# Second SBUF tensors of a router search turned into per-partition scalars, and two of its small results kept in PSUM

## The chip, the cores and the metric

The kernel runs on one core of a Trainium2 chip. The metric is the device time of one execution in microseconds (us), as the median of several runs. The engines are TensorE (PE; its weight loads are PEld), VectorE (DVE), ScalarE (ACT), GpSimd (POOL) and SyncE (SP, which issues DMAs).

## The reference

Three layers run one after the other over 8 x 576 = 4608 tokens of 512 numbers. The first is banded attention with 8 heads. The second is a mixture of 8 experts, in which each token goes to the expert with its largest logit. The third, with which the change has to do, is a balanced mixture: no expert takes more than 4608 / 8 = 576 tokens, and the (token, expert) pairs are taken in falling order of their logits:

```
logits = x @ w_gate
order = np.argsort(-logits.flatten())
for idx in order:
    tok, e = int(idx) // E, int(idx) % E
    if assigned[tok] >= 0 or counts[e] >= cap:
        continue
    assigned[tok] = e
    counts[e] += 1
for e in range(E):
    mask = assigned == e
    h = np.maximum(x[mask] @ w1[e], 0.0)
    out[mask] = h @ w2[e]
```

## The kernel before

The tokens' logits for the third layer lie in SBUF as `lg`, 128 partitions x 40 columns x 8 experts. The greedy order is not walked pair by pair. Instead the kernel searches, eight times, for the logit at which the next expert becomes full, and fixes that expert's tokens. One such round is a `Phase`, numbered k from 0 to 7, and has these parts:

- `head`: the largest logit of each token, `m`, over the experts still open (line 1253); where it stands, `eq` (line 1256); `m` is then pushed below everything for tokens already assigned by adding `pen` (line 1257); `eq` times `rvc` (line 1259) and a maximum give the chosen expert `rm`, and `oh` (line 1269) its one-hot form. `wt` (line 1265) holds the step widths.
- `search`, six steps: `edges` (line 1278) writes 32 thresholds `ed` into a PSUM tile "pg"; `cm` (line 1297) compares `m` with them in two pieces; TensorE counts with `cm` and `oh` (line 1308), adds over column groups (line 1317) and over experts (line 1323). VectorE turns the counts into the number `nb` of thresholds passed (line 1327) and the new lower end `lo` (line 1333). The upper end is `tighten`: lines 1283, 1284 and 1286 compute `q`, and line 1288 takes the minimum into `hi`. These last four are handed out one by one in the next step.
- `route` fixes the expert `code` and its mark `cl` (line 1381), and finds each token's place with two products on TensorE.
- `settle` takes the expert out: `remb` (lines 1417 and 1419) counts the room left. `slots` turns the places into the list `idx` of the expert's tokens (lines 1425 to 1459), with `rr` (lines 1436, 1442), `bl` (line 1440), a product into "pt" (line 1448), its copy `sv` (line 1451), and a second product (line 1454).

Phase 0 runs while the second layer ends. Phases 1 to 7 run inside the third layer's matrix products: expert j is computed by `job2(j)` while the search for a later expert goes on between its matmuls. The order is fixed when the program is built: a clock that counts matmul time (`CLK`) and the costs that each part yields decide after which matmul the next small instruction is placed, and each engine executes its own sequence in order. The weights of the third layer are split into two parts, `wh` on ScalarE (line 202) and `wl` on GpSimd (line 203, a subtraction of two SBUF tensors of 128 x 512). GpSimd also issues the gathers of token rows (line 275) and the scatters of results (line 1548). VectorE makes the low part of the hidden layer, `ht` (line 880), and of the gathered rows, `xtl` (line 844), between the pieces of the search.

Of the kernel before, what the change touches and what calls it, by code (L numbers as in the profile page):

```python
# [10 lines left out]
F32 = mybir.dt.float32  # L11
# [5 lines left out]
OP = mybir.AluOpType  # L17
AX = mybir.AxisListType
# [139 lines left out]
def kernel(  # L158
# [1033 lines left out]
    def route_tables():  # L1192
# [13 lines left out]
        G.tensor_scalar(KC[3], cs[:, None, C_IOTA:C_IOTA + 32].to_broadcast([128, C, 32]), -1.0, 1.0, op0=OP.mult, op1=OP.mult)  # L1206
        G.tensor_copy(KC[4], cs[:, C_ROW:C_ROW + C])

    class Phase:
        def __init__(self, k):  # L1210
            self.k, self.tiles, self.lo, self.late = k, {}, lo0[:, 1:2], iter(())
# [8 lines left out]
    def head(T, c0=0):  # L1220
        V, k = nc.vector, T.k
        T.lo, T.late = lo0[:, 1:2], iter(())
        wt = T([128, NSTEP], "wt")
        df = T([128, 1], "df")
        if k == 0:
            m, rm, oh = top, TOP["rm"], TOP["oh"]
            V.memset(hi, BIG)
            s2 = T([128, 2], "s2")
            V.tensor_reduce(s2[:, 0:1], lmax, axis=AX.X, op=OP.max)
            V.tensor_reduce(s2[:, 1:2], lmin, axis=AX.X, op=OP.min, negate=True)  # L1230
            yield VP, 150
            p = pm2.tile([128, 128], F32, name="pr")
            nc.tensor.transpose(p[0:2, :], s2, ident)
            yield PE, 100
            fs = list(best(c0, C))
            for f in fs[:2]:
                f()
            v2 = T([2, 1], "v2")
            V.tensor_reduce(v2, p[0:2, :], axis=AX.X, op=OP.max)
            dg = T([2, 2], "dg")  # L1240
            V.tensor_scalar(dg, ident[0:2, 0:2], v2, None, op0=OP.mult)
            yield VP, 500
            p = pm2.tile([128, 128], F32, name="pr")
            nc.tensor.matmul(p[:, 0:2], onef[0:2, :], dg, start=True, stop=True)
            yield PE, 20
            for f in fs[2:]:
                f()
            V.tensor_scalar(lo0, p[:, 0:2], -1.0, None, op0=OP.mult)
            V.tensor_scalar(df, p[:, 0:1], lo0[:, 1:2], NWAY / (NWAY - 1.0), op0=OP.subtract, op1=OP.mult)
        else:  # L1250
            rvc, rve = KC[0], KC[1]
            m = T([128, C], "m")
            V.tensor_reduce(m, lg, axis=AX.X, op=OP.max)
            yield V, 400
            eq = T([128, 8 * C], "eq", F16).rearrange("p (c e) -> p c e", e=8)
            V.tensor_tensor(eq, lg, bC8(m), op=OP.is_equal)
            V.tensor_tensor(m, m, pen, op=OP.add)  # L1257
            yield V, 470
            V.tensor_tensor(eq, eq, rvc[:, None, :].to_broadcast([128, C, 8]), op=OP.mult)
            V.tensor_scalar(df, hi, lo0[:, 1:2], None, op0=OP.subtract)  # L1260
            yield V, 340
            rm = T([128, C], "rm", F16)
            with nc.allow_low_precision(reason="small whole numbers"):
                V.tensor_reduce(rm, eq, axis=AX.X, op=OP.max)
        V.tensor_scalar(wt, cs[:, C_PW:C_PW + NSTEP], df, None, op0=OP.mult)
        yield V, 500
        if k:
            oh = T([128, 8, C], "oh2", F16)
            V.tensor_tensor(oh, rve, rm[:, None, :].to_broadcast([128, 8, C]), op=OP.is_equal)
            yield V, 240  # L1270
        T.m, T.rm, T.oh, T.wt = m, rm, oh, wt
        if k < 7:
            edges(T, 0)
            yield V, 110

    def edges(T, s):
        T.ed = pm2.tile([128, NWAY], F32, name="pg")
        nc.vector.tensor_scalar(T.ed, cs[:, C_IOTA:C_IOTA + NWAY], T.wt[:, s:s + 1], T.lo, op0=OP.mult, op1=OP.add)

    def tighten(T, nb, w, lo):  # L1280
        V = nc.vector
        q = T([128, 2], "q")
        V.tensor_scalar(q[:, 0:1], nb, 1.0, w, op0=OP.add, op1=OP.mult)
        V.tensor_scalar(q[:, 1:2], nb, NWAY - 1.5, BIG, op0=OP.is_ge, op1=OP.mult)
        yield V, 200
        V.scalar_tensor_tensor(q[:, 0:1], q[:, 0:1], lo, q[:, 1:2], op0=OP.add, op1=OP.add)
        yield V, 130
        V.tensor_tensor(hi, hi, q[:, 0:1], op=OP.min)

    def search(T, s):  # L1290
        V, k, lo, ed, m, oh, late = nc.vector, T.k, T.lo, T.ed, T.m, T.oh, T.late
# [38 lines left out]
            V.scalar_tensor_tensor(T.sat, p[:, 0:8], nb, rev8, op0=OP.is_equal, op1=OP.mult)  # L1330
        yield V, YN[0]
        lo2 = T([128, 1], f"lo{s % 2}")
        V.scalar_tensor_tensor(lo2, nb, w, lo, op0=OP.mult, op1=OP.add)  # L1333
        T.late, T.lo = tighten(T, nb, w, lo), lo2
        yield V, YN[1]
        if s < NSTEP - 1:
# [3 lines left out]
    def route(T):  # L1340
# [36 lines left out]
        tot = T([2 * C, 128], "tot", F16)  # L1377
        nc.scalar.copy(tot, p[0:2 * C, :])
        if k < 7:
            cl = T([128, 8], "cl")  # L1380
            V.tensor_scalar(cl, rev8, code, None, op0=OP.is_equal)
            yield V, 80
            ck = T([128, 8], "ck")
            V.tensor_scalar(ck, cl, -2.0 * BIG, BIG, op0=OP.mult, op1=OP.add)
            yield V, 250
        else:
            yield PE, 300
# [138 lines left out]
    def split2(k, half):  # L1526
        j, q = pieces[k]
        loads2(k)
        w2nd.split(j, q, half)
        if half:  # L1530
            nsp[0] += 1
            loads2()
# [267 lines left out]
    for q in range(QFIRST, 4):  # L1800
        for h in range(2):
            split2(q, h)
    t0 = CLK[0]
    while CLK[0] < t0 + AHEAD:
        advance(0)
# [26 lines left out]
```

## Time and profile before

| What | Value |
|---|---|
| Median of 3 runs | 1314.62 us (1313.16 to 1315.28) |
| The profiled execution, its own time | 1317.96 us |
| Its span, first to last instruction | 1316.2 us |
| PE busy | 1225.6 us (93%) |
| DVE busy | 910.1 us (69%) |
| POOL busy | 546.5 us (42%) |
| ACT busy | 502.8 us (38%) |
| Mean granted TensorE clock | 0.975 |

A share of busy time is a mean over three layers with different limits. To see what the search costs one has to look at the stretch in which it runs, at what TensorE waits for there, and at the instructions in front of those waits.

### The profile page before, as it was taken

How to read it: one execution, taken by the hardware profiler on the slowest of the kernel's cores; microseconds unless marked ns; L12 is line 12 of the kernel's file. 1: busy time of each engine (PE TensorE's matmuls, PEld its weight loads, DVE VectorE, ACT ScalarE, POOL GpSimd, SP SyncE). 2: the span in 40 equal slices, each digit the busy share in tenths (PEclk: the TensorE clock that was granted, in tenths of full speed). 3: DMA queues.
4: the chain of work that ended last, by engine and by line, in shares of the span. 5: the costliest groups of instructions: out<-in, count | busy, mean ns of one | idle time of the engine just before them, and what ended most of it. 6: DMA issues, size and time to landing. Idle time of an engine off the chain costs nothing. (4 is left out here: it accounts for less than half of the span.)

```text
span 1316.2 us, 25338 instructions
## 1 busy us (share of the span) xinstructions
PE 1225.6 (93%) x9286; PEld 1045.1 (79%) x9286; DVE 910.1 (69%) x2702; ACT 502.8 (38%) x1388; POOL 546.5 (42%) x682
## 2 busy tenths in 40 slices
PE   7999999898899999999999969999989999999996
PEld 6887888687798978888888748687878788788894
DVE  5777778757999999977966547677677776752120
ACT  4666666433233342334333123232323332333330
POOL 4232222236435362543634024454555454446431
PEclk9999999888999999999999989899999999999998
DMA  9977676255424352433520050505050515054101
GB/s 204 218 186 176 154 176 147 78 185 195 147 84 140 105 156 87 149 105 106 164 87 1 21 175 17 182 19 174 28 180 21 160 42 180 22 180 149 68 5 36
DMA packets 157746, 155.07 MB, mean 118 GB/s; under 512 B 74296, under 2 KB 123320, under 8 KB 157488
## 3 DMA queue, kind: packets, MB, share of 16 engines
q1 hardware_dynamic: 148656, 124.50, 33.0%
q0 software_dynamic: 8960, 28.89, 7.2%
q8 instruction: 76, 1.25, 0.4%
q14 instruction: 54, 0.44, 0.1%
HBM read 124.46 MB, written 28.90 MB: 117 GB/s over the span
## 5 line engine op out<-in xcount | busy, mean ns | idle before, releaser
L203 POOL TENSOR_TENSOR wl<-wst,wh 128x512 fp32r<-128x512 f32 x250 | 323.9, 1318 | 276.2 <-ACT wh L202 268.6
L874 PE MATMUL ph<-xth,wh 128*128 128x256 f32 (+5 forms) x1024 | 314.2, 307 | 21.1 <-DVE ht L880 20.2
L874 PE MATMUL ph<-xtl,wh 128*128 128x256 f32 (+5 forms) x1024 | 309.9, 303 | 0.3 <-DVE xtl L844 0.3
L874 PE MATMUL ph<-xth,wl 128*128 128x256 f32 (+5 forms) x1024 | 309.2, 302 | 0.0
L900 PE MATMUL py<-wh,ht 128*128 128x512 f32 (+2 forms) x848 | 282.0, 409 | 1.3 <-DVE jk L942 1.3
L878 ACT ACTIVATE ht<-ph 128x256 fp32r<-128x256 f32 (+5 forms) x256 | 106.7, 417 | 297.7 <-PE ph L874 297.5
L874 PEld LDWEIGHTS ph<-xth,wh 128*128 128x128 f32 x1024 | 194.9, 190 | 29.7 <-DVE ht L880 24.1
L880 DVE SCALAR_TENSOR_TENSOR ht<-ph,ht 128x256 fp32r<-128x256 f32 (+4 forms) x344 | 124.1, 382 | 107.8 <-ACT ht L878 103.5
L874 PEld LDWEIGHTS ph<-xtl,wh 128*128 128x128 f32 x1024 | 195.0, 190 | 2.4 <-DVE xtl L844 0.5
L874 PEld LDWEIGHTS ph<-xth,wl 128*128 128x128 f32 x1024 | 194.8, 190 | 1.5
L900 PEld LDWEIGHTS py<-wh,ht 128*128 128x128 f32 (+2 forms) x848 | 157.2, 190 | 39.4 <-issue 4.1
L900 PE MATMUL py<-wl,ht 128*128 128x512 f32 (+2 forms) x424 | 172.4, 407 | 0.0
L202 ACT CAST wh<-wst 128x512 fp32r<-128x512 f32 x256 | 148.1, 618 | 9.6 <-SPq L1638 5.9
L436 POOL TENSOR_TENSOR pr<-pr,st 128x384 f32<-128x384 f32 x68 | 56.2, 826 | 145.6 <-DVE st L434 82.4
L426 ACT ACTIVATE pr<-pS,st 128x96 f32<-128x96 f32 x288 | 94.2, 341 | 55.3 <-DVE st L430 26.7
L1548 POOL DMA_INDIRECT out_dram<-xo,tki x40 | 41.2, 1029 | 158.1 <-ACT xo L910 39.8
L844 DVE TENSOR_TENSOR xtl<-pt,xth 128x512 fp32r<-128x512 f32 (+1 forms) x78 | 50.0, 646 | 82.1 <-ACT xth L843 78.1
L900 PEld LDWEIGHTS py<-wl,ht 128*128 128x128 f32 (+2 forms) x424 | 80.7, 190 | 21.3 <-issue 3.2
L942 DVE SCALAR_TENSOR_TENSOR jk<-py,aux,wgb 128x512 f32<-128x512 f32 (+2 forms) x128 | 95.6, 747 | 2.8
L415 PEld LDWEIGHTS pS<-kt,qb 128*128 128x128 f32 x576 | 75.1, 195 | 8.3 <-POOL qb L629 2.9
L910 ACT COPY xo<-py 128x512 f32<-128x512 f32 (+1 forms) x40 | 23.4, 585 | 149.8 <-issue 73.4
L415 PE MATMUL pS<-kt,qb 128*128 128x96 f32 x576 | 75.6, 275 | 3.9 <-DVE qb L389 2.8
(310 smaller groups left out, 2006.8 us busy)
## 6 DMA issues: line engine op xcount, KB each, us to landing
wst<-in_moe_w_dram SPq DMA_DIRECT2D x132, 512.0 KB
x_d<-xo SPq DMA_DIRECT2D x34, 257.0 KB
x_d<-xr SPq DMA_DIRECT2D x8, 1028.0 KB
knp<-in_k_dram SPq DMA_DIRECT2D x32, 128.0 KB
qnp<-in_q_dram SPq DMA_DIRECT2D x32, 128.0 KB
vd<-in_v_dram SPq DMA_DIRECT2D x8, 384.0 KB
wgb<-wg_d SPq DMA_DIRECT2D x1, 2048.0 KB
vp<-in_v_dram SPq DMA_DIRECT2D x12, 168.0 KB
```

What stands on the lines that cost most here:

```text
L202: nc.scalar.copy(h[:, s], t[:, s])
L203: (self.eng0 if (j, q) in self.early else self.eng).tensor_tensor(l[:, s], t[:, s], h[:, s].bitcast(F32), op=OP.subtract)
L415: nc.tensor.matmul(p[:, u, :], QB[a][hp][:, 4 * g + u].rearrange("p h c -> p (h c)"), win, start=False, stop=True, skip_group_check=True)
L426: nc.scalar.activation(pr[:, u], sm[:, u], AF.Exp, bias=st[:, 1, u:u + 1], accum_out=st[:, 2, u:u + 1])
L436: eng.tensor_tensor(pr, pr, st[:, 3, :, None].to_broadcast([128, 4, 96]), op=OP.mult)
L844: nc.vector.tensor_sub(l[:, :, o], p[:, :, :m], h[:, :, o].bitcast(F32))
L874: nc.tensor.matmul(p[:, :n], a, b[:, c, o:o + n], start=(k == 0), stop=(k == 11))
L878: nc.scalar.activation(h.hi[:, o:o + n], p[:, :n], AF.Relu)
L880: nc.vector.scalar_tensor_tensor(lo, p[:, a - o:b - o], 0.0, h.hi[:, a:b].bitcast(F32), op0=OP.max, op1=OP.subtract)
L900: nc.tensor.matmul(p[:m], h.part[a][:, 128 * t:128 * t + m], w_, start=(f == 0 and w_ is wh and a == 0), stop=(f == 7 and w_ is wl))
L942: nc.vector.scalar_tensor_tensor(JK[e % 2][:m], a, s, WG["b"][:m, e], op0=OP.mult, op1=OP.mult, accum_out=lt[:m, e:e + 1])
L1548: st = nc.gpsimd.indirect_dma_start(out=out, out_offset=bass.IndirectOffsetOnAxis(ap=ti[:m], axis=0), in_=xo[:m, 0:DM], in_offset=None)
```

## The change

Three things are done, all of them on VectorE:

- `lo`, `q` and `hi` (lines 1333, 1286 and 1288) had one-element tensors as their second tensor. They become `tensor_scalar` instructions, in which the second operand is a scalar read per partition. This holds for all phases.
- One PSUM tile, `RS[0]`, takes the buffer "pg" when the third layer begins and keeps it to the end. For phases 1 to 7 the thresholds lie in it, in two halves that the steps use in turn, the maxima `m0` in columns 64 to 103, and the mark `cl` in columns 104 to 111. `m`, the sum with `pen`, stays in SBUF.
- So `eq` and `m` read `m0`, and `remb` reads `cl`, from PSUM.

```diff
@@ -1206,6 +1206,8 @@
         G.tensor_scalar(KC[3], cs[:, None, C_IOTA:C_IOTA + 32].to_broadcast([128, C, 32]), -1.0, 1.0, op0=OP.mult, op1=OP.mult)
         G.tensor_copy(KC[4], cs[:, C_ROW:C_ROW + C])
 
+    RS = []
+
     class Phase:
         def __init__(self, k):
             self.k, self.tiles, self.lo, self.late = k, {}, lo0[:, 1:2], iter(())
@@ -1249,12 +1251,12 @@
             V.tensor_scalar(df, p[:, 0:1], lo0[:, 1:2], NWAY / (NWAY - 1.0), op0=OP.subtract, op1=OP.mult)
         else:
             rvc, rve = KC[0], KC[1]
-            m = T([128, C], "m")
-            V.tensor_reduce(m, lg, axis=AX.X, op=OP.max)
+            m, m0 = T([128, C], "m"), RS[0][:, 64:64 + C]
+            V.tensor_reduce(m0, lg, axis=AX.X, op=OP.max)
             yield V, 400
             eq = T([128, 8 * C], "eq", F16).rearrange("p (c e) -> p c e", e=8)
-            V.tensor_tensor(eq, lg, bC8(m), op=OP.is_equal)
-            V.tensor_tensor(m, m, pen, op=OP.add)
+            V.tensor_tensor(eq, lg, bC8(m0), op=OP.is_equal)
+            V.tensor_tensor(m, m0, pen, op=OP.add)
             yield V, 470
             V.tensor_tensor(eq, eq, rvc[:, None, :].to_broadcast([128, C, 8]), op=OP.mult)
             V.tensor_scalar(df, hi, lo0[:, 1:2], None, op0=OP.subtract)
@@ -1274,7 +1276,8 @@
             yield V, 110
 
     def edges(T, s):
-        T.ed = pm2.tile([128, NWAY], F32, name="pg")
+        o = NWAY * (s % 2)
+        T.ed = RS[0][:, o:o + NWAY] if T.k else pm2.tile([128, NWAY], F32, name="pg")
         nc.vector.tensor_scalar(T.ed, cs[:, C_IOTA:C_IOTA + NWAY], T.wt[:, s:s + 1], T.lo, op0=OP.mult, op1=OP.add)
 
     def tighten(T, nb, w, lo):
@@ -1283,9 +1286,9 @@
         V.tensor_scalar(q[:, 0:1], nb, 1.0, w, op0=OP.add, op1=OP.mult)
         V.tensor_scalar(q[:, 1:2], nb, NWAY - 1.5, BIG, op0=OP.is_ge, op1=OP.mult)
         yield V, 200
-        V.scalar_tensor_tensor(q[:, 0:1], q[:, 0:1], lo, q[:, 1:2], op0=OP.add, op1=OP.add)
+        V.tensor_scalar(q[:, 0:1], q[:, 0:1], lo, q[:, 1:2], op0=OP.add, op1=OP.add)
         yield V, 130
-        V.tensor_tensor(hi, hi, q[:, 0:1], op=OP.min)
+        V.tensor_scalar(hi, hi, q[:, 0:1], None, op0=OP.min)
 
     def search(T, s):
         V, k, lo, ed, m, oh, late = nc.vector, T.k, T.lo, T.ed, T.m, T.oh, T.late
@@ -1330,7 +1333,7 @@
             V.scalar_tensor_tensor(T.sat, p[:, 0:8], nb, rev8, op0=OP.is_equal, op1=OP.mult)
         yield V, YN[0]
         lo2 = T([128, 1], f"lo{s % 2}")
-        V.scalar_tensor_tensor(lo2, nb, w, lo, op0=OP.mult, op1=OP.add)
+        V.tensor_scalar(lo2, nb, w, lo, op0=OP.mult, op1=OP.add)
         T.late, T.lo = tighten(T, nb, w, lo), lo2
         yield V, YN[1]
         if s < NSTEP - 1:
@@ -1377,7 +1380,7 @@
         tot = T([2 * C, 128], "tot", F16)
         nc.scalar.copy(tot, p[0:2 * C, :])
         if k < 7:
-            cl = T([128, 8], "cl")
+            cl = RS[0][:, 64 + C:72 + C] if k else T([128, 8], "cl")
             V.tensor_scalar(cl, rev8, code, None, op0=OP.is_equal)
             yield V, 80
             ck = T([128, 8], "ck")
@@ -1800,6 +1803,7 @@
     for q in range(QFIRST, 4):
         for h in range(2):
             split2(q, h)
+    RS.append(pm2.tile([128, 512], F32, name="pg"))
     t0 = CLK[0]
     while CLK[0] < t0 + AHEAD:
         advance(0)
```

The change moves no instruction: each engine's sequence is the one of before, with other operands on VectorE. Two places show it. The first is VectorE in the head of phase 2, behind the product "pt" that `sv` copies; the names are those of the list above, and `po`, `df` and `kpad` are small helpers. Before:

```order
L1419 SCALAR_TENSOR_TENSOR remb<-cl,remb 128x8
L1253 TENSOR_REDUCE m<-lg 128x40
L1256 TENSOR_TENSOR eq<-lg,m 128x320
L1257 TENSOR_TENSOR m<-m,pen 128x40
L1451 CAST sv<-pt 128x36
L1259 TENSOR_TENSOR eq<-eq,rvc 128x320
L1260 TENSOR_SCALAR df<-hi,lo_4042 128x1
L1456 TENSOR_TENSOR kpad<-pt,cs 128x2x18
```

The same engine at the same place, after:

```order
L1422 SCALAR_TENSOR_TENSOR remb<-pg,remb 128x8
L1255 TENSOR_REDUCE pg<-lg 128x40
L1258 TENSOR_TENSOR eq<-lg,pg 128x320
L1259 TENSOR_TENSOR m<-pg,pen 128x40
L1454 CAST sv<-pt 128x36
L1261 TENSOR_TENSOR eq<-eq,rvc 128x320
L1262 TENSOR_SCALAR df<-hi,lo_4042 128x1
L1459 TENSOR_TENSOR kpad<-pt,cs 128x2x18
```

Nothing moved: `remb`, `eq` and `m` read "pg", which is PSUM, where they read `cl` or `m` in SBUF, and `sv` stands behind `m` as before.

The second place is VectorE in a search step of phase 1, inside the products of the first expert (`ht` belongs to them). Before:

```order
L1319 TENSOR_TENSOR flg<-pr,remb 32x8
L1286 SCALAR_TENSOR_TENSOR q<-q,lo_4042 128x1
L880 SCALAR_TENSOR_TENSOR ht_10460<-ph,ht_10460 128x256
L880 SCALAR_TENSOR_TENSOR ht_10460<-ph,ht_10460 128x64
L1288 TENSOR_TENSOR hi<-hi,q 128x1
L1327 TENSOR_REDUCE nb_10723<-pr 128x1
L1333 SCALAR_TENSOR_TENSOR lo_10728<-nb_10723,wt,lo_10631 128x1
L1278 TENSOR_SCALAR pg<-cs,wt,lo_10728 128x32
L1297 TENSOR_TENSOR cm<-m,pg 128x640
```

The same step, after:

```order
L1322 TENSOR_TENSOR flg<-pr,remb 32x8
L1289 TENSOR_SCALAR q<-q,lo_4042 128x1
L880 SCALAR_TENSOR_TENSOR ht_10461<-ph,ht_10461 128x256
L880 SCALAR_TENSOR_TENSOR ht_10461<-ph,ht_10461 128x64
L1291 TENSOR_SCALAR hi<-hi,q 128x1
L1330 TENSOR_REDUCE nb_10722<-pr 128x1
L1336 TENSOR_SCALAR lo_10727<-nb_10722,wt,lo_10631 128x1
L1281 TENSOR_SCALAR pg<-cs,wt,lo_10727 128x32
L1300 TENSOR_TENSOR cm<-m,pg 128x640
```

Again nothing moved: `q`, `hi` and `lo` have another form, and `cm` still follows two rows behind `lo`.

## Rows read from the trace of the kernel before

**Rows 1.** Busy us by stretch: PE, PEld, DVE, ACT, POOL; clock, DMA, GB/s.

```profile
785.00:1195.00 410.00, 387.58 (x2835) 321.36 (x2833) 282.34 (x837) 133.46 (x274) 201.40 (x225) 0.98 0.32 103
846.90:853.70 6.80, 5.80 (x15) 4.59 (x15) 4.15 (x12) 0.00 (x0) 4.65 (x5) 0.50 0.82 266
...
918.60:922.00 3.40, 3.40 (x9) 2.25 (x8) 2.25 (x5) 1.62 (x3) 2.97 (x3) 0.50 0.79 242
976.60:980.00 3.40, 3.40 (x10) 2.63 (x9) 1.89 (x4) 0.00 (x0) 2.52 (x3) 0.50 0.79 247
```

**Rows 2.** Waits of PE, 785 to 1200: us in total, times, longest us.

```profile
PE pt L1454 <- DVE sv L1451: 6.4, 4, 2.9
PE pr L1308 <- DVE cm L1297: 4.3, 5, 1.3
PE ph L874 <- DVE ht L880: 2.6, 5, 1.6
PE pt L1448 <- DVE rr L1442: 2.5, 2, 1.3
...
PE pr L1375 <- DVE mm L1371: 0.9, 2, 0.7
PE pt L840 <- DMA xrow<-x_d,idx: 0.6, 1, 0.6
PE ph L874 <- ACT ht L878: 0.6, 1, 0.6
```

**Rows 3.** Timeline, POOL and DVE, two steps of phase 1: start us, us.

```profile
808.46 1.28 POOL L203 TENSOR_TENSOR wl<-wst,wh 128x512 fp32r<-128x512 f32 x1 [1.30 <-ACT wh L202]
...
808.64 1.12 DVE L1333 SCALAR_TENSOR_TENSOR lo<-nb,wt,lo 128x1 f32<-128x1 f32 x1
...
812.28 1.29 POOL L203 TENSOR_TENSOR wl<-wst,wh 128x512 fp32r<-128x512 f32 x1 [0.48 <-ACT wh L202]
...
812.65 0.20 DVE L1283 TENSOR_SCALAR q<-nb,wt 128x1 f32<-128x1 f32 x1
```

**Rows 4.** Instructions of one line: duration ns min/median/max, first and last start us.

```profile
L1333 DVE SCALAR_TENSOR_TENSOR lo<-nb,wt,lo x42: 204/219/3150, 740.2 to 1147.3; 128x1 f32<-128x1 f32 x42
...
L1283 DVE TENSOR_SCALAR q<-nb,wt x42: 196/204/208, 742.3 to 1148.5; 128x1 f32<-128x1 f32 x42
...
L1265 DVE TENSOR_SCALAR wt<-cs,df x8: 220/223/3225, 735.8 to 1163.7; 128x6 f32<-128x6 f32 x8
```

**Rows 5.** Timeline, head of phase 2; in brackets idle before and its releaser.

```profile
845.19 2.48 POOL L203 TENSOR_TENSOR wl<-wst,wh 128x512 fp32r<-128x512 f32 x2
...
844.75 3.00 DVE L1257 TENSOR_TENSOR m<-m,pen 128x40 f32<-128x40 f32 x1
...
842.95 0.91 PE L1448 MATMUL pt<-rr,bl 128*32 128x36 f16 x40
...
847.90 0.19 PE L1454 MATMUL pt<-sv,kmod 128*128 128x36 f16 x1 [2.92 <-DVE sv L1451]
...
849.57 1.55 DVE L1297 TENSOR_TENSOR cm<-m,pg 128x640 f16<-128x640 f32 x2
...
854.61 0.42 PE L1308 MATMUL pr<-oh,cm 128*128 128x32 f16 x10
```

**Rows 6.** Timeline, head of phase 3, DVE and PE.

```profile
906.20 3.06 DVE L1419 SCALAR_TENSOR_TENSOR remb<-cl,remb 128x8 f32<-128x8 f32 x1
...
916.11 0.29 PE L1308 MATMUL pr<-oh,cm 128*128 128x32 f16 x5 [1.29 <-DVE cm L1297]
916.84 0.29 PE L1308 MATMUL pr<-oh,cm 128*128 128x32 f16 x5 [0.44 <-DVE cm L1297]
```

**Rows 7.** Timeline, head of phase 1, DVE and PE.

```profile
791.93 1.17 DVE L1257 TENSOR_TENSOR m<-m,pen 128x40 f32<-128x40 f32 x1
793.02 0.33 DVE L1259 TENSOR_TENSOR eq<-eq,rvc 128x320 f16<-128x320 f16 x1
...
794.62 0.38 PE L874 MATMUL ph<-xth,wh 128*128 128x256 f32 x1 [1.57 <-DVE ht L880]
```

## The prediction, made before the changed kernel ran

> **What bounds the kernel now.** I read the busy time by stretch first. The change touches only the search that hands tokens to the eight experts of the last layer, and seven of the eight searches run between 785 and 1195 us, spread between the matrix products. There TensorE is busy for 387.58 of 410 us [rows 1]. So TensorE sets the pace, and some 22 us of the stretch are its waits. What a faster search is worth is what it takes out of these waits, and no more.
>
> Second I read what TensorE waited for there [rows 2]. VectorE ends most of it: the cast sv 6.4 us in four waits, the comparison cm 4.3 in five, ht 2.6 in five, rr 2.5, mm 0.9, and 0.6 behind ScalarE's ht. So VectorE's short instructions, although VectorE is not full, decide when TensorE goes on: they are executed in order, and one that is held holds everything behind it.
>
> Third I read two engines side by side [rows 3]. A GpSimd subtraction wl begins at 808.46 and takes 1.28, to 809.74. VectorE's one-element lo begins at 808.64 and takes 1.12, to 809.76: it ends when GpSimd does. Over its 42 executions lo has a median of 0.219 us and a maximum of 3.150 [rows 4]. Nothing in lo is long; it is held for as long as GpSimd runs, and at the maximum through several GpSimd operations in a row. What lo has in common with the other held ones (q, hi, m, remb, eq) is two tensors read from SBUF. Instructions that read one tensor from SBUF are not held: q at line 1283 begins at 812.65, inside a wl that runs from 812.28 for 1.29 us, and takes 0.20 [rows 3]; its maximum over 42 is 0.208 [rows 4].
>
> **The change part by part.** The order of instructions on every engine stays as it was; only operands change.
>
> *lo, q, hi in the search loop* (42 of each) keep one tensor, and the second becomes a per-partition scalar. The row that shows this form, output and operands alike, is line 1283, with no hold in 42. So I take the holds of these three at nothing. What TensorE waits for them: the cm waits near 1118 to 1127, that is 4.3 less the 1.29 and 0.44 of [rows 6], 2.6; the ht waits less the 1.57 of [rows 7], 1.0; mm 0.9; ScalarE's ht 0.6. Term (a): 2.6 + 1.0 + 0.9 + 0.6 = **5.1 us**.
>
> *m0, eq, m and cl in the head of a search.* The maximum m0 and the mark cl go to PSUM, so eq, m and remb read one SBUF tensor each. In the head of the third search, phase 2, VectorE's m is held 3.00 us from 844.75, while GpSimd runs wl until 847.67. Behind m stands the cast sv, whose input TensorE finished at 843.86 (842.95 + 0.91), and TensorE waits 2.92 us for sv [rows 5]. In the next head remb is held 3.06 us from 906.20 [rows 6], and sv is late again. All four sv waits stand behind one of these instructions. With the hold gone sv waits only for its input, which is there. Term (b): **6.4 us**.
>
> *wt, which the change does not touch*, is held once, for 3.225 us [rows 4], in the same head as that remb, and costs cm waits of 1.29 and 0.44 [rows 6]. With remb's hold of 2.9 us gone from in front of it, wt comes before the GpSimd operations that now catch it. Term (c): **1.7 us**.
>
> *TensorE's clock.* It is granted 0.50 (1.2 instead of 2.4 GHz) in stretches of 6.80, 3.40 and 3.40 us that follow the waits of three heads [rows 1]. A half-clock stretch costs half its length, 3.4, 1.7 and 1.7, if TensorE is what is late there. After the first it isn't for long: TensorE reaches the matmuls on cm at 854.61; without the 2.92 wait and the 3.4 that is 848.3, while cm ends at 851.12 [rows 5]. Without the wait alone it is 851.7, so the clock adds 0.6 there. The second head gives its whole 1.7, the third I count at nothing. Term (d): **2.3 us**, with 4.0 at the upper end.
>
> *What the change adds.* A store or load in PSUM instead of SBUF in a head, and a scalar load in hi. The nearest rows bound this: a maximum of 0.208 for the scalar form against 0.219 for lo before [rows 4] gives a gain of 0.01, and lo's median taken as the price of a whole extra access would be 0.2 us for each of some three instructions in seven heads, 4 us. I take nothing, because TensorE has products in its queue while a head runs (between 842.95 and its wait it issued them for two microseconds), and keep 4 us as an end. RS holds one PSUM buffer to the end; nothing else in the order takes that buffer after it.
>
> *What is given back.* Instructions with two SBUF tensors remain (line 1259's eq times rvc, oh, rr, bl, asg), and wt too can be held. The new timing throws them against GpSimd again. I leave (c)'s 1.7 in as the price of such new meetings, and another 1.7 for waits under 0.15 us that stay where each of some 17 waits is taken away (an estimate, 0.1 us each). Term (e): **-3.4 us**.
>
> Sum: 5.1 + 6.4 + 1.7 + 2.3 - 3.4 = 12.1 us. The profiled execution took 1317.96 us, 1.8 us outside its span of 1316.2; the median of the runs is 1314.62. The gain comes off either: 1305.9 for a profiled execution, **1302.5** for the median.
>
> **The rivals.**
>
> *The scalar form is held as well.* lo, q and hi would still wait for wl, and only the heads gain: 6.4 + 1.7 + 2.3 - 3.4 = 7.0, so 1307.6. For it: wt, a scalar form from SBUF to SBUF with six elements, was held once, to 3.225 us [rows 4]. Against it: line 1283 with one element, never in 42. The Trainium skill has a rule for this side: "VectorE: DVE Perf Modes", section "What auto-detection actually checks", says that an operation with one source runs through both ports if source and destination lie in SBUF and their outermost sizes are both even or equal, and "SBUF — State Buffer", section "Who interferes with whom", that such an operation contends with GpSimd. [...]
>
> *The hold moves to the next instruction.* In the head of phase 1 m is held from 791.93 for 1.17, and right behind it line 1259, which still has two SBUF tensors, starts at 793.02, when GpSimd is done; TensorE then waits 1.57 for ht [rows 7]. Without m's hold line 1259 takes the same hold, and the wait stays: I have not counted this 1.57. If it were so in all heads, with sv's partners caught too, (b) to (d) would vanish and (e) with them: 5.1 gained, 1309.5. Against it: sv stands ahead of line 1259.
>
> *Something else takes the time.* TensorE would be early at the gathered rows, which GpSimd issues after idx, and wait there. The gain would go to nothing: 1314.6. For it: one such wait of 0.6 us is there now. Against it: it is one in seven heads [rows 2].
>
> *Slower.* VectorE, no longer delayed, could arrive with rr (line 1442) or line 1259 just as a run of two wl begins, and with it sv and cm behind them. The largest price in the trace is TensorE's 2.92 wait in one head [rows 5]. It would have to fall in six of the seven heads (6 x 2.92 = 17.5) to undo the 15.5 of (a) to (d); in all seven it gives 1314.62 - 15.5 + 20.4 = 1319.5. For it: rr alone costs 2.5 us now [rows 2]. Against it: that is two meetings in seven heads, not six.
>
> **How the numbers follow.** Forecast 0.66; the hold moves 0.14; scalar form held 0.08; no gain 0.06; slower 0.06. The forecast's top is 5.1 + 6.4 + 1.7 + 4.0 = 17.2, which gives 1297.4; its bottom takes the 4 us of PSUM and scalar cost, 1306.5. The range runs to the two weaker gains, 1297 to 1310, and leaves out the last two cases and a little of the first. What a measurement of this kernel can tell from no change is about 0.2%, 2.6 us. Faster by more than that: 0.66 + 0.14 + 0.08 = 0.88; within it 0.06; slower 0.06.
>
> **What would show it.** In the changed kernel lo, q and hi should keep a maximum near 0.21 us, and m and remb too; if they reach 1 us, the first rival holds. The sv waits should be gone or below 1 us together, the clock should be 1.00 in at least two of the three half-clock stretches, and line 1259 should show a maximum well above its neighbours where it takes over a hold. The forecast is wrong if TensorE's waits between the first and last head stay near 22 us although the holds are gone: then they were not what TensorE waited for.

## The result, and the profile after

| | Before | After |
|---|---|---|
| Median, same chip | 1313.89 us (1308.44 to 1315.28, 4 runs) | 1294.01 us (1292.07 to 1295.02, 4 runs) |
| Ratio, 95% interval | | 0.9855 (0.9832 to 0.9879) |
| The profiled execution, its span | 1317.96, 1316.2 us | 1295.02, 1293.3 us |

The kernel became 19.9 us faster. The forecast was 12.1 us, 1302.5 with a range of 1297 to 1310: the direction and the holds were right, but the gain came out 7.8 us larger, and the time fell 3 us below the range. The kernel before took 1314.62 us when the forecast was made and 1313.89 here, which is 0.7 of these 3 us.

The page of the changed kernel, its span and its busy times:

```profile
span 1293.3 us, 25338 instructions
...
PE 1217.4 (94%) x9286; PEld 1040.6 (80%) x9286; DVE 881.7 (68%) x2702; ACT 503.4 (39%) x1388; POOL 545.8 (42%) x682
```

VectorE is busy 28.4 us less, for the same number of instructions: most of that is held time that is gone. The stretch of the seven searches (columns as in [rows 1]; the second row is the head of phase 2, the third that of phase 4):

```profile
785.00:1195.00 410.00, 399.74 (x2969) 336.38 (x2969) 256.88 (x850) 141.22 (x293) 213.73 (x237) 0.99 0.33 109
...
841.90:845.30 3.40, 3.40 (x33) 2.53 (x23) 2.68 (x9) 1.75 (x4) 3.09 (x5) 1.00 1.05 402
...
964.00:976.00 12.00, 11.22 (x73) 7.76 (x72) 6.72 (x21) 3.65 (x7) 10.29 (x13) 1.00 0.49 167
```

TensorE fills 399.74 of 410 us where it filled 387.58, and both heads, which were followed by 0.50 in [rows 1], run at 1.00. What TensorE still waits for, in the view of [rows 2]:

```profile
PE ph L874 <- DVE ht L880: 3.4, 1, 3.4
PE pt L840 <- DVE xtl L844: 2.0, 2, 1.2
PE pt L1451 <- DVE rr L1445: 1.9, 2, 1.3
PE pr L1311 <- DVE cm L1300: 1.2, 3, 0.4
PE pr L1378 <- DVE mm L1374: 0.8, 4, 0.3
PE pt L840 <- DMA xrow<-x_d,idx: 0.7, 1, 0.7
...
```

Lines past 1208 have moved by two or three: `lo` is now 1336, `q` 1286 to 1289, `hi` 1291, `m` 1259, `eq` times `rvc` 1261, `wt` 1267, `sv` 1454. The row of `sv` with its 6.4 us is gone. The instructions themselves, in the view of [rows 4]:

```profile
L1336 DVE TENSOR_SCALAR lo<-nb,wt,lo x42: 264/272/276, 736.3 to 1126.8; 128x1 f32<-128x1 f32 x42
...
L1289 DVE TENSOR_SCALAR q<-q,lo x42: 251/252/274, 740.1 to 1127.8; 128x1 f32<-128x1 f32 x42
...
L1291 DVE TENSOR_SCALAR hi<-hi,q x42: 202/214/216, 740.4 to 1128.1; 128x1 f32<-128x1 f32 x42
...
L1259 DVE TENSOR_TENSOR m<-pg,pen x7: 190/191/193, 790.3 to 1141.6; 128x40 f32<-128x40 f32 x7
...
L1422 DVE SCALAR_TENSOR_TENSOR remb<-pg,remb x6: 152/156/158, 840.9 to 1140.0; 128x8 f32<-128x8 f32 x6
...
L1261 DVE TENSOR_TENSOR eq<-eq,rvc x7: 313/316/1045, 790.5 to 1141.8; 128x320 f16<-128x320 f16 x7
...
L1267 DVE TENSOR_SCALAR wt<-cs,df x8: 218/222/2280, 731.9 to 1142.6; 128x6 f32<-128x6 f32 x8
```

Everything that the change touched has minimum and maximum together; what it left with two SBUF tensors, and `wt`, still has executions that are held. The head of phase 2, which [rows 5] shows before:

```profile
840.86 0.15 DVE L1422 SCALAR_TENSOR_TENSOR remb<-pg,remb 128x8 f32<-128x8 f32 x1
...
841.98 0.19 DVE L1259 TENSOR_TENSOR m<-pg,pen 128x40 f32<-128x40 f32 x1
842.25 0.20 DVE L1454 CAST sv<-pt 128x36 f16<-128x36 f32 x1
...
844.14 2.02 DVE L1267 TENSOR_SCALAR wt<-cs,df 128x6 f32<-128x6 f32 x1
...
846.65 1.55 DVE L1300 TENSOR_TENSOR cm<-m,pg 128x640 f16<-128x640 f32 x2
...
848.26 0.29 PE L1311 MATMUL pr<-oh,cm 128*128 128x32 f16 x5 [0.44 <-DVE cm L1300]
```

`m` takes 0.19 instead of 3.00 us and `sv` comes at once. The next instruction that GpSimd holds is `wt`, 2.02 us, and TensorE has enough queued to lose 0.44 to it.

**Where the time went.** For every trace I took the time between the same two matmuls (those that begin at 788.5 and 1195.3 us in the trace of before; each trace has the same 9286), and from the records of TensorE its idle gaps above 0.15 us and the time at a granted clock of 0.50. If a half-clock stretch costs half its length, the rest (stretch less waits less half of the half-clock time) should not depend on the kernel:

| Kernel | Stretch | Waits | Half-clock time | Rest |
|---|---|---|---|---|
| before, two traces | 406.8, 406.2 | 21.2, 22.4 | 17.1, 13.7 | 377.1, 377.0 |
| after, four traces | 390.3, 386.0, 387.2, 385.2 | 10.6, 9.0, 9.1, 8.4 | 6.8, 0.3, 3.4, 0.0 | 376.3, 376.9, 376.4, 376.7 |
| scalar forms alone | 397.1 | 16.3 | 10.2 | 375.7 |
| PSUM operands alone | 393.1 | 12.4 | 3.6 | 378.9 |

The rest is 375.7 to 377.1 in all but one, the PSUM operands alone, which stays unexplained. The factor of a half can be read from the traces too: over all fifteen traces without idle matmuls, those of the experiments below included, a straight line through stretch less waits against half-clock time has a slope of 0.50, with a standard error of 0.05. That is what TensorE's own work loses; what would be late in its place is not in it. By means, the stretch became 19.3 us shorter (406.5 to 387.2): 12.5 from waits (21.8 to 9.3), 6.4 from the clock (half of 15.4 less half of 2.6), and 0.5 that these leave. Outside the stretch the first two traces differ by another 4.4 us before it and 2.0 behind it. These belong to the execution and not to the change: over the traces of all kernels below the matmul at 788.5 begins between 780.8 and 790.7 us, in an order that follows no edit.

### The profile page after: what moved, and what is told of

Its sections match the earlier page's. It is cut to its first block, busy times and chain, and to the rows that moved or that the text cites. A ratio compares the mean times of both kernels' runs of the same rounds, so it can differ in the third digit from the quotient of the medians.

```text
span 1293.3 us, 25338 instructions
## 1 busy us (share of the span) xinstructions
PE 1217.4 (94%) x9286; PEld 1040.6 (80%) x9286; DVE 881.7 (68%) x2702; ACT 503.4 (39%) x1388; POOL 545.8 (42%) x682
## 5 line engine op out<-in xcount | busy, mean ns | idle before, releaser
L900 PE MATMUL py<-wh,ht 128*128 128x512 f32 (+2 forms) x848 | 277.7, 404 | 1.3 <-DVE jk L942 1.3
L874 PEld LDWEIGHTS ph<-xth,wh 128*128 128x128 f32 x1024 | 194.8, 190 | 25.5 <-DVE ht L880 21.2
```

The costliest lines, as they stand in the source:

```text
L874: nc.tensor.matmul(p[:, :n], a, b[:, c, o:o + n], start=(k == 0), stop=(k == 11))
L900: nc.tensor.matmul(p[:m], h.part[a][:, 128 * t:128 * t + m], w_, start=(f == 0 and w_ is wh and a == 0), stop=(f == 7 and w_ is wl))
```

## Experiments

Each series of runs shares one chip and its own runs of the kernel before; a ratio is always against those.

**The same kernels again.** No edit.

> The kernel before, once more, for a second trace of it. Between its two profiled executions and the one of the changed kernel, TensorE's matmuls come 3.9 us earlier in the changed kernel already at 735 us, ahead of every instruction that the change can reach in time. If that is a property of the single execution (theory), this trace stands 2 us or more away from the first trace of before at 735 us, in either direction, while the stretch from 785 to 1195 us takes the same 410 us within 3. If the change causes it in some way (rival), both traces of before agree at 735 us within 0.5 us.

Measured: one run, 1313.95 us, stretch 406.2 us. At the matmul at 735 us the two traces of before differ by 0.4 us, which by this expectation speaks for the rival; at 500 to 600 us they differ by 2.8. Other traces settle it: the two kernels with idle matmuls below are the kernel before up to that place, and the matmul comes at 731.4 and 731.3 us in them, where the first trace of after has 731.2. So the earlier start is not an effect of the change.

> The changed kernel, beside its two halves on one chip. Both theories: 0.983 to 0.988 of the kernel before. It is the measure for the two halves below.

Measured: 1292.86, ratio 0.9862 (0.9836 to 0.9889). Twice more, in later series:

> The changed kernel on the chip of this call, for the two versions beside it: 0.984 to 0.988 of before.

> The changed kernel, on the chip of the two versions beside it: 0.984 to 0.988 of before.

Measured: 1292.51, ratio 0.9854 (0.9831 to 0.9877), and 1298.21, ratio 0.9853 (0.9829 to 0.9877; there before itself took 1317.92). The gain is 17 to 20 us in four series.

**One half at a time.** The three scalar forms alone (before with these lines):

```diff
-        V.scalar_tensor_tensor(q[:, 0:1], q[:, 0:1], lo, q[:, 1:2], op0=OP.add, op1=OP.add)
+        V.tensor_scalar(q[:, 0:1], q[:, 0:1], lo, q[:, 1:2], op0=OP.add, op1=OP.add)
...
-        V.tensor_tensor(hi, hi, q[:, 0:1], op=OP.min)
+        V.tensor_scalar(hi, hi, q[:, 0:1], None, op0=OP.min)
...
-        V.scalar_tensor_tensor(lo2, nb, w, lo, op0=OP.mult, op1=OP.add)
+        V.tensor_scalar(lo2, nb, w, lo, op0=OP.mult, op1=OP.add)
```

> Only lo, q and hi changed to the scalar form; m, eq and cl stay in SBUF. Theory (every instruction with two SBUF tensors is held while GpSimd runs, and nothing else matters): lo, q and hi never exceed 0.28 us, m and remb still reach about 3 us, the four sv waits stay near 6 us in all, and the gain is that of the search loop with some clock, 5 to 9 us (ratio 0.993 to 0.996). Rival (the holds of the heads alone cost time, those in the loop hide behind matmuls): within 2.6 us of before.

Measured: 1301.03, ratio 0.9933 (0.9908 to 0.9958). TensorE's waits, the duration of `lo` and `m`, and the stretches behind the heads of phases 2 and 4:

```profile
PE pt L1454 <- DVE sv L1451: 6.4, 4, 2.9
...
PE pr L1308 <- DVE cm L1297: 1.7, 2, 1.3
```

```profile
L1333 DVE TENSOR_SCALAR lo<-nb,wt,lo x42: 264/272/276, 734.1 to 1131.5; 128x1 f32<-128x1 f32 x42
...
L1257 DVE TENSOR_TENSOR m<-m,pen x7: 199/202/3003, 785.3 to 1146.5; 128x40 f32<-128x40 f32 x7
```

```profile
841.90:845.30 3.40, 3.40 (x10) 2.61 (x9) 2.00 (x4) 0.00 (x0) 2.65 (x3) 0.50 0.84 256
964.80:968.20 3.40, 3.40 (x9) 2.63 (x8) 2.81 (x8) 0.00 (x0) 2.21 (x3) 0.50 0.74 198
```

`cm` fell by exactly the 2.6 of term (a), `sv` kept its 6.4, and the half clock behind both heads stayed with it.

The PSUM operands alone (after with the three lines above undone):

> Only the PSUM half: m0, eq, m and cl and the thresholds in the kept PSUM tile; lo, q and hi keep two SBUF tensors. Theory: m and remb never exceed 0.25 us and the sv waits fall below 1 us in all, lo, q and hi are still held up to 1 to 3 us; the gain is that of the heads with their clock, 9 to 13 us (ratio 0.990 to 0.993), and the two halves add up to the whole within 4 us. Rival (a hold that is taken away comes back at the next instruction with two SBUF tensors): under 5 us, and the two halves together are well short of the whole.

Measured: 1301.21, ratio 0.9936 (0.9911 to 0.996). No row of `sv`; `lo` is held as before:

```profile
PE pr L1311 <- DVE cm L1300: 3.7, 6, 1.2
```

```profile
L1336 DVE SCALAR_TENSOR_TENSOR lo<-nb,wt,lo x42: 204/220/3157, 737.5 to 1130.8; 128x1 f32<-128x1 f32 x42
```

The second half alone stays a little under the 9 to 13 us expected. The halves bring 8.6 and 8.4 us (from 1309.59), 17.0 together, and the whole 16.7 in the same series: they add up as far as intervals of about 3 us each can tell, and neither needs the other. By the stretch, one trace each, they bring 9.4 and 13.4, together 3.5 more than the 19.3 of the whole.

**One held instruction put back.** After, with the first `q` given a second SBUF tensor:

```diff
-        V.tensor_scalar(q[:, 0:1], nb, 1.0, w, op0=OP.add, op1=OP.mult)
+        V.scalar_tensor_tensor(q[:, 0:1], nb, 1.0, w, op0=OP.add, op1=OP.mult)
```

> The changed kernel with one instruction turned the other way: the first q of tighten (line 1283 of before), which had one SBUF tensor in both kernels and was never held, gets its step width as a second SBUF tensor. Work and result stay the same. Theory (two SBUF tensors against a running GpSimd are what holds): its 42 executions, never above 0.21 us before, are held about ten times, for 0.5 to 3 us, and 1 to 4 us of the gain are lost (ratio 0.987 to 0.990 to before). Rival (the form or the place of lo, q and hi mattered, not the number of SBUF tensors): maximum stays below 0.3 us and the time is that of the changed kernel, 0.986.

Measured: 1300.39, ratio 0.9894 (0.9876 to 0.9912), 4 to 5 us of the gain gone (against the ratios of 0.9853 to 0.9862 of after in other series), although this `q` is faster when nothing holds it:

```profile
L1286 DVE SCALAR_TENSOR_TENSOR q<-nb,wt x42: 142/152/3806, 743.6 to 1134.0; 128x1 f32<-128x1 f32 x42
```

Its longest execution on the timeline (start us, us), with GpSimd beside it and TensorE behind it:

```profile
972.39 3.81 DVE L1286 SCALAR_TENSOR_TENSOR q<-nb,wt 128x1 f32<-128x1 f32 x1
...
976.18 0.14 DVE L1322 TENSOR_TENSOR flg<-pr,remb 32x8 f16<-32x8 f32 x1
...
972.34 2.50 POOL L203 TENSOR_TENSOR wl<-wst,wh 128x512 fp32r<-128x512 f32 x2
974.78 0.18 POOL L847 COPY kp<-xrow 128x2 f32<-128x2 f32 x1
974.92 1.25 POOL L203 TENSOR_TENSOR wl<-wst,wh 128x512 fp32r<-128x512 f32 x1
...
976.38 0.16 PE L1326 MATMUL pr<-flg,one 33*128 33x8 f16 x1 [2.35 <-DVE flg L1322]
```

A one-element instruction starts 0.05 us after a run of GpSimd work and ends when the run ends, at 976.2; `flg` stands behind it and TensorE waits 2.35 us. This is the whole mechanism in six rows: one operand in one line makes the difference, and the place where TensorE pays is the next of VectorE's results that it needs.

**Is it the form or the number of SBUF tensors?** After with the old two-tensor forms, but `nb`, the flag and the sum of `q` in the PSUM tile:

```diff
+        qc, qb = (RS[0][:, 116:117], RS[0][:, 117:118]) if T.k else (q[:, 0:1], q[:, 1:2])
...
-        V.tensor_scalar(lo2, nb, w, lo, op0=OP.mult, op1=OP.add)
+        V.scalar_tensor_tensor(lo2, nb, w, lo, op0=OP.mult, op1=OP.add)
```

> The changed kernel with the old instruction forms of lo, q and hi, but their second tensor in PSUM (nb, the flag and the sum of q lie in the kept tile). It tells the scalar form from the number of SBUF tensors. Theory: lo, q and hi are not held in this form either, maximum below 0.3 us, and the time is that of the changed kernel within 2 us. Rival (only the scalar form escapes): they reach 1 us or more and the time is near that of the PSUM half alone, 0.993.

Measured: 1291.44, ratio 0.9839 (0.9823 to 0.9855). `lo` in phases 1 to 7:

```profile
L1337 DVE SCALAR_TENSOR_TENSOR lo<-pg,wt,lo x36: 208/218/219, 800.6 to 1125.5; 128x1 f32<-128x1 f32 x36
```

The two-tensor instruction isn't held either, once one of its tensors lies in PSUM. So for these instructions what counts is how many tensors come from SBUF (`wt`, which has one and is held all the same, is another case: see the next experiment). The Trainium skill says the same ("SBUF — State Buffer", section "Who interferes with whom": a VectorE instruction with two SBUF inputs contends with a GpSimd instruction that reads SBUF), and the traces agree: in the trace of before, 21 executions of `lo`, `q` and `hi` (lines 1333, 1286 and 1288) start while a `wl` runs; 19 of them take 0.9 to 2.5 us, and the other two, of 0.20 and 0.21, start in its last 0.2 us. In this kernel 11 of the 36 `lo` start so, and none takes over 219 ns.

**What the remaining holds cost.** After, with `rvc` and `wt` in the PSUM tile as well:

```diff
-        wt = T([128, NSTEP], "wt")
+        wt = RS[0][:, 130:130 + NSTEP] if T.k else T([128, NSTEP], "wt")
...
-            rvc, rve = KC[0], KC[1]
+            rvc, rve = RS[0][:, 120:128], KC[1]
```

> The changed kernel, with two more operands of the head in the kept PSUM tile: rvc, so that eq times rvc reads one SBUF tensor, and wt, so that it is written to PSUM. Theory: neither of the two exceeds 0.4 us any more (they reached 1.0 to 1.8 and 2.3 us), TensorE's wait in the head of phase 1 (1.5 and 3.4 us in the two traces of the changed kernel) falls by 1 us or more, and the kernel gains 1 to 3 us on the changed one. Rival (the hold moves on to oh, the next instruction with two SBUF tensors): oh shows a maximum above 1 us and the time stays within 1 us.

Measured: 1289.26, ratio 0.9813 (0.98 to 0.9827). The hold moved to the next instruction with two SBUF tensors, `oh`:

```profile
L1261 DVE TENSOR_TENSOR eq<-eq,pg x7: 477/478/486, 792.1 to 1143.2; 128x320 f16<-128x320 f16 x7
...
L1271 DVE TENSOR_TENSOR oh<-rve,rm x7: 315/317/2016, 793.2 to 1145.5; 128x320 f16<-128x320 f16 x7
```

`wt`, now 216 to 220 ns in phases 1 to 7, is held no more. TensorE's wait for `ht` in the head of phase 1, expected to fall by 1 us or more, is 3.60 us in this trace, and the stretch takes 390.1 us, within the 385.2 to 390.3 of after. The same kernel again, beside after:

> Once more rvc and wt in the PSUM tile, now with the changed kernel beside it. Before it stood at 0.981 of its own call and the changed kernel at 0.985 and 0.986 in others. Theory (the holds left at line 1259 and at wt still cost something): 1 to 4 us below the changed kernel. Rival (they hide, the difference was one of calls): within 1 us of it.

Measured: 1295.75, ratio 0.9839 (0.9816 to 0.9863), 2.5 us below after in that series (0.9853, 0.9829 to 0.9877): not told apart; its stretch is 385.2 us. With the forms of the experiment before added:

> rvc and wt in the PSUM tile, and lo, q and hi in their old forms with the second operand in PSUM. Theory (each SBUF tensor taken from a two-tensor instruction takes away a hold, and the old forms are 0.05 us shorter than the scalar ones): 0.5 to 5 us below the changed kernel, ratio 0.980 to 0.984. Rival (what is left now is another hold, of line 203 on VectorE in the head of phase 1): within 1 us of the changed kernel.

Measured: 1293.97, ratio 0.9861 (0.983 to 0.9892), beside 1292.51 of after in that series: no gain. And with `krow`, the second tensor of `rr`, in PSUM too:

```diff
-        V.tensor_tensor(ah, ah, krow[:, None, :].to_broadcast([128, NHI, C]), op=OP.mult)
+        V.tensor_tensor(ah, ah, (RS[0][:, 140:140 + C] if k else krow)[:, None, :].to_broadcast([128, NHI, C]), op=OP.mult)
```

> The same version with krow in the PSUM tile too, so that rr times krow reads one SBUF tensor; with a 4-byte second operand the instruction gets longer, from 0.53 to about 0.9 us. Theory (the two rr waits of TensorE, 2.5 us in all, are holds): no execution of it exceeds 1 us, the rr waits fall below 1 us, and the kernel gains 1 to 2 us on the version without. Rival (its own 0.4 us more in seven heads cost as much): within 1 us of that version.

Measured: 1296.25, ratio 0.9829 (0.9802 to 0.9855), 2 us below after in the same series, again not told apart. `rr` is never held, TensorE's waits for it fall from 1.9 to 2.6 us in after's traces to 0.6, and the stretch has 7.6 us of waits:

```profile
L1445 DVE TENSOR_TENSOR rr<-rr,pg x7: 892/893/905, 841.8 to 1153.4; 128x720 f16<-128x720 f16 x7
```

So beside after in one series these versions lie 2.5 us below it, 1.5 above and 2 below, never told apart. The first run of 0.9813 would be 5 to 6 us below after, but that stands in another series, and its own trace shows no shorter stretch. What the holds that the change left are worth is not shown; the runs point to 2 to 3 us or nothing.

**VectorE's own `wl`.** In the head of phase 1 of after, VectorE's share of the weight split (line 203, two SBUF tensors) is held while GpSimd runs its own, 4.86 us for two pieces that took 1.28 in the trace of before, and `ht` comes late by 3.43 us, the largest wait that is left:

```profile
784.64 4.86 DVE L203 TENSOR_TENSOR wl<-wst,wh 128x512 fp32r<-128x512 f32 x2
...
786.44 2.52 POOL L203 TENSOR_TENSOR wl<-wst,wh 128x512 fp32r<-128x512 f32 x2
...
792.06 0.39 PE L874 MATMUL ph<-xth,wh 128*128 128x256 f32 x1 [3.43 <-DVE ht L880]
```

That piece given to GpSimd, on top of the kernel with both sets of edits:

```diff
-    w2nd = Weights(w21, w22, nc.gpsimd, nc.vector, ((0, 0), (0, 2)))
+    w2nd = Weights(w21, w22, nc.gpsimd, nc.vector, ((0, 0),))
```

> The version before this one in the list, with the one quarter of the first expert's weights that VectorE splits in the head of phase 1 (the third quarter) split by GpSimd as all others. VectorE's subtraction has two SBUF tensors and was held up to 3.3 us there. Theory: TensorE's wait for ht in the head of phase 1 (3.1 to 3.6 us in three traces) falls below 1.6 us, gain 1 to 3 us. Rival (GpSimd's queue is the bound there): the first products wait for wl instead, and the time grows by 1 to 3 us.

Measured: 1292.38, ratio 0.9861 (0.9837 to 0.9886), beside 1293.97 of the version without: not told apart, and TensorE's wait is 2.55 us where less than 1.6 was expected. The hold moves to `oh`, which stands ahead of the same `ht`:

```profile
783.73 3.85 DVE L1271 TENSOR_TENSOR oh<-rve,rm 128x320 f16<-128x320 f16 x1
787.50 0.41 DVE L880 SCALAR_TENSOR_TENSOR ht<-ph,ht 128x256 fp32r<-128x256 f32 x1
...
782.41 4.98 POOL L203 TENSOR_TENSOR wl<-wst,wh 128x512 fp32r<-128x512 f32 x4
...
787.97 0.39 PE L874 MATMUL ph<-xth,wh 128*128 128x256 f32 x1 [2.55 <-DVE ht L880]
```

GpSimd runs four pieces of `wl` there, 4.98 us, and the first instruction with two SBUF tensors that stands in that head takes the rest of it.

**The clock by itself.** Before, with idle matmuls in front of the product on `sv`, so that TensorE stays busy while it waits for `sv`:

```diff
+        for _ in range({1: 50, 2: 14, 3: 34, 4: 10}.get(k, 0)):
+            nc.tensor.matmul(p, one16, iot16, start=True, stop=True)
```

A first version had the same counts at phases 2 to 5, one head too late.

> The kernel before, with idle matmuls (128 columns, results unread) in front of the product on sv in four heads: 50, 14, 34 and 10 in phases 2 to 5, about as long as TensorE's waits there. No wait is taken away, only TensorE is busy in it. It measures the clock's share by itself. Theory (the half-clock stretches follow the waits, and they are the part of the gain that the forecast made too small): the half-clock stretches between 785 and 1195 us, 17.0 and 13.6 us in the two traces of before, shrink below 8 us, and the time falls by 2 to 4 us. Rival (the clock falls for another reason, the waits alone made the gain): the stretches stay, and the time stays or grows by up to 1 us.

Measured: 1313.22, ratio 1.0008 (0.9997 to 1.002); by its misplacement it decides little.

> The kernel before with idle matmuls again, now in front of the product on sv where TensorE waits: the lists of phases 1, 2, 3 and 4 are made in the heads of phases 2, 3, 4 and 5, so the 50, 14, 34 and 10 matmuls stood one head too late. Theory (the half-clock stretches follow the idle TensorE): the sv waits fall from 6.4 us to below 1 us without any hold being taken away, the half-clock stretches between 785 and 1195 us shrink from 17.0 and 13.6 us below 7, and the stretch gets 2 to 5 us shorter. Rival (the clock does not follow these waits): the half-clock stretches stay, and the stretch takes the same 406 us.

Measured: 1312.98, ratio 1.001 (0.9991 to 1.0029). The head of phase 2, and the clock behind it and behind that of phase 4:

```profile
845.16 2.97 PE L1455 MATMUL pt<-iot,one 128*128 128x128 f16 x50
848.26 0.18 PE L1456 MATMUL pt<-sv,kmod 128*128 128x36 f16 x1
```

```profile
846.00:853.00 7.00, 6.86 (x69) 5.74 (x66) 5.59 (x13) 1.53 (x4) 4.95 (x6) 1.00 0.91 305
970.00:985.00 15.00, 14.00 (x138) 10.70 (x137) 11.79 (x23) 4.26 (x9) 12.01 (x14) 1.00 0.73 235
```

With the idle matmuls in the wait, the half clock behind both heads is gone. In this one trace three others stand elsewhere, 6.8 us each, at waits of 3.34, 4.22 and 1.15 us that weren't filled, so that the stretch has 20.5 us at half clock and 412.7 us in all. So the waits for `sv` went as expected, but the half-clock time grew where less than 7 us was expected, and the stretch got longer where it was to get 2 to 5 us shorter; this execution, of 1317.81 us, is the slowest of the twelve. The experiment shows, in one trace, what the clock falls behind, and doesn't price it: the time didn't move, and since VectorE is as late as before, TensorE waits for it elsewhere.

## Why the prediction was right in kind and short in size

The time lies outside the range. The step that failed is term (d), the clock: it was sized at 2.3 us and measured 6.4, because TensorE was bounded by a `cm` that stood behind the removed hold itself, and because one half-clock stretch was put at nothing without a reason. Term (e) was too large as well, 3.4 us against 0.7. The terms one by one:

**(a) search loop, 5.1 us: right, 4.3 measured.** `lo`, `q` and `hi` have maxima of 276, 274 and 216 ns. Gone are the `cm` waits near 1118 to 1127 (2.6), four of the five `ht` waits (1.0) and ScalarE's `ht` (0.6); `mm` has 0.8 us in four short waits where it had 0.9 in two. That is 4.3 us. One reading was wrong: line 1283, taken as the form of all three, has one per-partition scalar, while `lo` and `q` now have two, so that the 0.01 us gained per execution is 0.05 lost (last section).

**(b) heads, 6.4 us: right.** The `sv` row is gone, and only with the PSUM operands.

**(c) `wt`, 1.7 us: right in the head that it spoke of.** In the head of phase 3 `wt` started at 911.52 in the kernel before, inside a GpSimd operation that began at 911.14; now it comes ahead of that operation, and the two `cm` waits there are gone:

```profile
903.21 0.22 DVE L1267 TENSOR_SCALAR wt<-cs,df 128x6 f32<-128x6 f32 x1
903.85 1.00 POOL L1551 DMA_INDIRECT out_dram<-xo,tki  x1 [1.69 <-ACT wh L202]
```

In this trace `wt` is held in two other heads instead, of phases 2 and 4 (2.02 and 2.28 us), and `cm` waits 1.2 us behind it there; that belongs to (e). In the kernel with `wt` in PSUM a single `cm` wait of 0.4 is left.

**(d) the clock, 2.3 us with 4.0 at the upper end: mis-sized, 6.4 measured.** Two steps failed. The first head's half clock was to cost 0.6 of its 3.4, because "`cm` ends at 851.12" stops TensorE anyway. But that `cm` stood on VectorE behind the very hold of `m` that term (b) removed: I had moved TensorE and left VectorE where it was. Counted from the product that `sv` copies (842.95 before [rows 5], 841.30 after), `cm` ended 8.17 us behind it in the kernel before and 6.90 in the changed one, although `wt` was held in front of it there; TensorE began its matmuls on `cm` 11.66 us behind it and 6.23. That is 5.4 us, the wait of 2.92 and 2.5 more. The third stretch, counted at nothing without a reason, was the second failed step: it is in both traces of before, and in none of after, and is worth 1.7. Against that, the second head's 1.7 was counted whole, and its stretch stands in one of the two traces of before only; and a stretch behind two waits for `xtl`, which I left out (first row: before, columns as in [rows 1]; second: after), is in both traces of before (3.4 and 6.8 us) and still in two of the four of after (3.4 us each):

```profile
864.00:867.40 3.40, 3.40 (x25) 3.19 (x26) 1.20 (x5) 0.37 (x1) 0.00 (x0) 0.50 0.01 1
```

```profile
857.20:860.60 3.40, 3.40 (x26) 3.24 (x24) 1.04 (x5) 0.37 (x1) 3.08 (x8) 0.52 0.20 77
```

By means over the traces the three heads make 5.1 of the 6.4 (2.5, 0.9 and 1.7, against 0.6, 1.7 and 0 in the forecast). The stretch behind `xtl` makes 1.7, which isn't shown to come from the change, and the head of phase 1 takes 0.4 back. The 6.4 rests on the accounting above, with its slope of 0.50, and not on a time: the direct test with idle matmuls did not price the clock.

**(e) given back, -3.4 us: too large, -0.7 measured** (13.2 for (a) to (c) less 12.5; -2.6 by the first two traces). New meetings did happen: `eq` times `rvc` is held up to 1045 ns in the first trace and up to 2842 in two others, `wt` up to 2280, VectorE's two `wl` are 3.6 us longer than before. But `sv` stands ahead of most of them and TensorE has products queued. What comes back is 1.2 at `cm`, 0.8 at `mm`, and in the first trace 1.9 more at `ht`. The other part of the term, 1.7 us for waits under 0.15 us, does not show: such waits would lie in the rest, which did not grow but fell by 0.5.

Together: 12.5 + 6.4 against 13.2 + 2.3 - 3.4, 6.8 us too little, of which (d) made 4.1 and (e) 2.7. The other 1.0 of the 7.8 us is the 0.5 that the accounting leaves and 0.5 outside the stretch, too little to tell from noise. The best end of the range had (e) at nothing and the clock at 4.0, which is 17.2; with the clock at the 6.4 measured it would have been 19.6, or 1295.0 us, 1 us above the measured time.

**The rivals.** *Scalar form held*: fell, 0 of 42. *The hold moves*: right for the head of phase 1 in three of the four traces of after, where TensorE still waits for `ht` (1.3 to 3.4 us; 0.4 in the fourth): `eq` times `rvc` takes the hold in two of them (1.76 us), VectorE's `wl` in the other, `oh` in the kernel without that `wl`. In the other heads `sv` stands ahead and is free, and the rival's price of (b) to (d) did not come. *Something else takes the time*: the gathers' wait is 0.7 us, where it was 0.6. *Slower*: `rr` still costs 1.9 us, where it cost 2.5, and nothing of the kind happens in six heads.

## What to carry to other kernels

Compare median and maximum of the small instructions on an engine that runs beside GpSimd: where the maximum is far above the median (here 3150 ns against 219 for `lo`), the number of operands in SBUF is the first thing to change, a scalar pointer or a PSUM operand for one of them, and the gain is where TensorE waits for something behind the held one. When a hold is taken out of an in-order engine, move everything behind it by the same amount before asking what is late next; I bounded TensorE by an instruction that itself stood behind the hold. And a wait removed from TensorE can bring back more than its length, since a low granted clock follows some waits (here 0.50 for 3.4 or 6.8 us behind the wait of 2.92 us).

## What the runs showed of the hardware that was not expected

- A hold doesn't end with one GpSimd instruction: the `q` above was held 3.81 us through a `wl` pair, a copy and another `wl`. In one place of the trace of before it may go the other way: line 1436, with two SBUF tensors, starts 0.03 us behind a `wl` at 966.66 and takes its usual 0.53 us, and that `wl` takes 1.71 us where the median is 1.29; no run tests this.
- The scalar forms are slower when nothing holds them: `lo` 219 to 272 ns, `q` 198 to 252, `hi` 160 to 214 (medians), about 0.05 us each; no run shows this in the time. The medians of these one-element instructions go by the number of per-partition scalars: 144 to 160 ns with none (line 1284, the old `hi`), 198 to 219 with one (line 1283, the old `q` and `lo`, the new `hi`), 252 and 272 with two (the new `q` and `lo`). From the trace of before:

```profile
L1284 DVE TENSOR_SCALAR q<-nb x42: 135/144/151, 742.4 to 1148.6; 128x1 f32<-128x1 f32 x42
```

- A scalar form from SBUF to SBUF is held with six elements (`wt`, to 2280 ns) and was never held with one (maximum 276); with its output in PSUM `wt` isn't held either (216 to 220).
- Reading a 4-byte operand from PSUM was free for `eq` and `m` (492 to 486 and 202 to 191 ns), but dear where both SBUF operands had been f16: `eq` times `rvc` 315 to 478, `rr` times `krow` 526 to 893. The Trainium skill has a rule for it ("VectorE: DVE Perf Modes", section "The perf-mode tier table"): a two-tensor operation reaches its double rate on 16-bit tensors in SBUF, and not with any operand in PSUM; these two rows agree in direction, at 1.5 and 1.7 times, though there the operand became 4 bytes wide as well.
- The half clock behind the head of phase 2 stood in all four traces in which the wait for `sv` was left there (two of before, the scalar forms, the first fill), over 3.4 or 6.8 us, and in none where it was gone or filled.
